# Strassen's seven block products for the first expert product of a fused attention and expert kernel

## The chip, the cores and the metric

One core of one Trainium2 chip runs the whole program in one launch. The metric is the device time of one execution in microseconds (us). Everything is float32; matrix products are exact to about float32 by splitting each operand into a high part (rounded to fp32r, the type that TensorE multiplies) and a low part (the rest), and summing three products: high by low, low by high, high by high.

## The reference

```
x = attention(q, k, v, memory)            # [1152, 512]
h = (x @ w1) * (x @ w2);  x2 = h @ w3 @ w_out   # [1152, 512]
p = probs / probs.sum(-1);  out = 0
for e in range(4):                        # all four experts, every token
    out += p[:, e:e+1] * (relu(x2 @ e_w1[e]) @ e_w2[e])   # 512 -> 1024 -> 512
```

## The kernel before

Tokens are columns: activations are held transposed, features on the 128 partitions, tokens along the free axis, 2 batches of 576 tokens. A first stage (attention, and beside it the product w3 @ w_out) ends in `xT`. `BUnits` (one object per batch) computes (x @ w1) * (x @ w2) in 16 units into `hT`, 8 tiles of 128 features; its matmuls are called `ab` in the trace. `c_unit` multiplies `hT` by the combined weights `Wt` (trace name `c`, 24 matmuls per unit) and evicts: ScalarE copies the high part out of PSUM, VectorE subtracts for the low part (`lo_dve`). Batch 0 goes to `x2a`, batch 1 to `x2b`. The matmuls of batch 1's `ab` and `c` are mixed by the scheduler: a `c` can start on each tile of `hT` that is done.

The expert loop (lines 611 to 660) takes, per expert, three chunks of 512, 384 and 256 tokens (`CHUNKS`). In a chunk the first product (line 622, trace name `d`) makes 8 tiles of 128 hidden features, each from 4 feature blocks by 3 passes (`PASSES`), 12 matmuls; line 628 (ScalarE, relu) and line 629 (VectorE, low part) evict each into `he`. The second product (line 639, trace name `o`) takes 128 tokens at a time as the stationary operand: 8 hidden tiles by 3 passes, 24 matmuls of 512 columns; line 646 or 648 scales by the routing weight and adds to `acc`. Expert weights are loaded once per expert by the DMA queue of SP (line 554), and GpSimd (POOL) makes their high part (`hi_pool`, line 79) and low part (`lo_pool`, line 82). The order on each engine is chosen by the framework's scheduler; each engine then runs its own list in order.

```
for wi, xi in PASSES:
    nc.tensor.matmul(ps, lhsT=ew1[m // 4 * 4 + kk][:, wi, ...], rhs=rhs[:, xi, :], ...)   # L622
nc.scalar.activation(ht[:, 0, :], ps, AF.Relu)                                          # L628
nc.vector.scalar_tensor_tensor(out=ht[:, 1, :], in0=ps, scalar=0.0, in1=r32(ht[:, 0, :]), ...)  # L629
```

Of the kernel before, what the change touches and what calls it, by code (L numbers as in the profile page):

```python
# [33 lines left out]
def kernel(  # L34
# [451 lines left out]
    x2a = [main.tile([P, 2, S], F32R, tag=f"g{d}", name=f"x2a{d}") for d in range(KD)]  # L486
    x2b = []
# [11 lines left out]
    def c_unit(b, d, a, new_ps):  # L499
        st = {}  # L500

        def mm(k0, k1):
            def f():
                if k0 == 0:
                    st["ps"] = new_ps(d, a)
                for kk in range(k0, k1):
                    for x, (wi, xi) in enumerate(PASSES):
                        nc.tensor.matmul(  # L508
                            st["ps"][:, 0:HS], lhsT=Wt[kk][:, wi, d * P : (d + 1) * P],
                            rhs=hT[kk][:, xi, a * HS : (a + 1) * HS],  # L510
                            start=(kk == 0 and x == 0), stop=(kk == KF - 1 and x == 2),
                        )
                if k1 == KF:
                    x2, t0 = (x2b[d], S - CA + a * HS) if b else (x2a[d], a * HS)
                    cut = min(max(C2 - t0, 0), HS) if b else HS
                    for p0, p1, at in ((0, cut, t0), (cut, HS, t0 + cut + SHIFT)):
                        if p0 < p1:
                            ps = st["ps"][:, p0:p1]
                            nc.scalar.copy(x2[:, 0, at : at + p1 - p0], ps)
                            lo_dve(x2[:, 1, at : at + p1 - p0], ps, x2[:, 0, at : at + p1 - p0])  # L520
            return f

        return [mm(k, k + 2) for k in range(0, KF, 2)]

    def ps_main(d, a):
        return psM.tile([P, 512], F32, tag=f"M{a}", name=f"c0_{d}_{a}", bufs=1)
# [16 lines left out]
    fills += spread(C_SLOTS, [c_unit(0, d, a, ps_main) for d in range(KD) for a in range(2)])  # L543
# [8 lines left out]
    def load_tile(pool, rawp, src, tag, nm):  # L552
        r = rawp.tile([P, 512], F32, tag="re", name=f"r{nm}", bufs=3)
        nc.sync.dma_start(out=r, in_=src)
        t = pool.tile([P, 2, 512], F32R, tag=tag, name=nm)
        hi_pool(t[:, 0, :], r)
        lo_pool(t[:, 1, :], r, t[:, 0, :])
        return t

    def load_e1(pool, rawp, e, tag):  # L560

        return [
            load_tile(
                pool, rawp, e_w1[e, k * P : (k + 1) * P, g * 512 : (g + 1) * 512], f"{tag}{4 * g + k}", f"el1{e}_{g}_{k}"
            )
            for g in range(2) for k in range(KD)
        ]
# [26 lines left out]
    pB = p3.enter_context(tc.tile_pool(name="pB", bufs=1, side="left"))  # L594
    ph = p3.enter_context(tc.tile_pool(name="ph", bufs=9, side="left"))
    acc = [main.tile([P, 2, DM], F32, tag=f"g{KD + t}", name=f"acc{t}") for t in range(4)]
    acc.append(pB.tile([P, 1, DM], F32, name="acc4"))
    acc = [acc[t // 2][:, t % 2, :] for t in range(NTT)]
# [8 lines left out]

    groups = [(px, "v"), (main, "u"), (pB, "w")]
    ew2 = load_e2(main, px, 0, "u")
    ng = 2  # L610
    for e in range(E):
        nxt = None
        for c, (c0, cw) in enumerate(CHUNKS):
            hs = []
            x0 = c0 - CA + (SHIFT if c == 2 else 0)
            for m in range(KF):
                ps = ps3.tile([P, 512], F32, tag="P", name=f"d{e}_{c}_{m}")[:, 0:cw]
                n = 0
                for kk in range(KD):
                    rhs = x2a[kk][:, :, c0 : c0 + cw] if c0 < CA else x2b[kk][:, :, x0 : x0 + cw]  # L620
                    for wi, xi in PASSES:
                        nc.tensor.matmul(  # L622
                            ps, lhsT=ew1[m // 4 * 4 + kk][:, wi, m % 4 * P : (m % 4 + 1) * P],
                            rhs=rhs[:, xi, :], start=(n == 0), stop=(n == 3 * KD - 1),
                        )
                        n += 1
                ht = ph.tile([P, 2, 512], F32R, tag="he", name=f"he{e}_{c}_{m}")[:, :, 0:cw]
                nc.scalar.activation(ht[:, 0, :], ps, AF.Relu)  # L628
                nc.vector.scalar_tensor_tensor(  # L629
                    out=ht[:, 1, :], in0=ps, scalar=0.0, in1=r32(ht[:, 0, :]),  # L630
                    op0=ALU.max, op1=ALU.subtract,
                )
                hs.append(ht)
            for tt in range(cw // P):
                po = ps3.tile([P, 512], F32, tag="P", name=f"o{e}_{c}_{tt}")
                n = 0
                for kk in range(KF):
                    for xi, wi in PASSES:
                        nc.tensor.matmul(  # L639
                            po, lhsT=hs[kk][:, xi, tt * P : (tt + 1) * P], rhs=ew2[kk][:, wi, :],  # L640
                            start=(n == 0), stop=(n == 3 * KF - 1),
                        )
                        n += 1
                t = c0 // P + tt
                if e == 0:
                    nc.vector.tensor_scalar_mul(acc[t], po, pr[:, t, e : e + 1])
                else:
                    nc.vector.scalar_tensor_tensor(  # L648
# [47 lines left out]
```

## Time and profile before

| what | us |
|---|---|
| median of 3 runs (lowest to highest) | 757.91 (757.47 to 757.96) |
| the profiled execution's own time | 757.62 |
| its span, first to last instruction | 755.8 |
| TensorE (PE) busy | 737.1, 98% of the span |
| VectorE (DVE), ScalarE (ACT), GpSimd (POOL) busy | 283.9, 235.2, 224.9 |
| expert stage, first `d` matmul to last `o` | 355.87 to 751.69 |

A busy figure is the sum of an engine's instruction times. PE's pipelined matmuls overlap, so its spacing is read from the chain of waits: a stretch of so many matmuls by so many microseconds.

### The profile page before, as it was taken

Reading aid. Unit: us, or ns where it says so; the run is one execution under the profiler, and the core shown is the slowest. Engines: PE = TensorE matmul, PEld = TensorE weight load, DVE = VectorE, ACT = ScalarE, POOL = GpSimd, SP = SyncE. Lnnn points to the kernel's source line nnn. Section 1 sums busy time; section 2 is a strip of 40 time slices with the busy share of each in tenths; the row PEclk is TensorE's granted clock in tenths of the full one; section 3 lists DMA queues with packets and bytes.
Section 4 is the critical chain, followed back from the end, with each engine's and each line's share of the span. In section 5 each row is a group of like instructions: output and inputs, shape, how many; then the busy total and the mean of one; then the engine's idle time right before and its main releaser. Section 6 shows DMA issues by size and latency. Waiting matters only on the chain.

```text
span 755.8 us, 11259 instructions
## 1 busy us (share of the span) xinstructions
PE 737.1 (98%) x4568; PEld 656.1 (87%) x4568; DVE 283.9 (38%) x630; ACT 235.2 (31%) x475; POOL 224.9 (30%) x228
## 2 busy tenths in 40 slices
PE   3899999999999999999999999999999999999997
PEld 2778888899999999999889898898988899888986
DVE  6987557567744125332312122121221212121221
ACT  7976557565734323332201011010111011010110
POOL 2174543544540027003930077000590003400000
PEclk9999999999999999999999999999999999999999
DMA  9873313444511014101420033000131001101010
GB/s 274 277 223 114 105 49 111 146 142 127 180 47 29 2 55 154 56 29 23 138 65 1 1 98 126 0 1 1 57 128 39 1 1 31 39 1 56 0 42 29
DMA packets 48755, 56.69 MB, mean 75 GB/s; under 512 B 15808, under 2 KB 32192, under 8 KB 48704
## 3 DMA queue, kind: packets, MB, share of 16 engines
q1 hardware_dynamic: 48704, 55.97, 24.0%
q8 instruction: 36, 0.59, 0.3%
q14 instruction: 15, 0.12, 0.0%
HBM read 49.41 MB, written 6.55 MB: 74 GB/s over the span
## 4 chain that ended last, share of the span: by engine, by line
PE 92%; ACT 3%; DVE 2%; issue 1%; DMA 0%; POOL 0%; SPq 0%; DVEq 0%; ACTq 0%
PE d L622 26%; PE o L639 26%; PE ab L445 14%; PE c L508 7%; PE a L270 6%; PE wacc L380 5%; PE pt L257 3%; PE sc L217 3%; PE b L294 1%; ACT P L230 1%; PE x L313 1%; DVE tf_l L107 1%; DMA qd<-in_qT_dram 0%; DVE tf_wo L107 0%; ACT tu_l L104 0%
## 5 line engine op out<-in xcount | busy, mean ns | idle before, releaser
L639 PE MATMUL o<-el,he 128*128 128x512 f32 x864 | 198.2, 389 | 0.0
L639 PEld LDWEIGHTS o<-el,he 128*128 128x128 f32 x864 | 161.8, 188 | 33.4
L628 ACT ACTIVATE he<-d 128x512 fp32r<-128x512 f32 (+2 forms) x96 | 47.2, 492 | 337.2 <-PE d L622 337.2
L79 POOL TENSOR_SCALAR el<-rel 128x512 fp32r<-128x512 f32 x64 | 40.3, 636 | 255.5 <-PE d L622 186.3
L622 PE MATMUL d<-x2b,el 128*128 128x384 f32 (+1 forms) x768 | 113.8, 309 | 0.0
L622 PEld LDWEIGHTS d<-x2b,el 128*128 128x128 f32 x768 | 113.2, 188 | 0.6
L445 PE MATMUL ab<-xT,ws 128*128 128x288 f32 x768 | 113.2, 298 | 0.0
L629 DVE SCALAR_TENSOR_TENSOR he<-d,he 128x512 fp32r<-128x512 f32 (+2 forms) x96 | 53.6, 558 | 146.0 <-ACT he L628 146.0
L445 PEld LDWEIGHTS ab<-xT,ws 128*128 128x128 f32 x768 | 104.0, 188 | 1.8 <-ACT P L230 0.2
L622 PE MATMUL d<-x2a,el 128*128 128x512 f32 x384 | 87.7, 389 | 0.0
L622 PEld LDWEIGHTS d<-x2a,el 128*128 128x128 f32 x384 | 72.0, 188 | 14.9
L82 POOL TENSOR_TENSOR el<-rel,el 128x512 fp32r<-128x512 f32 x64 | 83.1, 1314 | 1.8
L648 DVE SCALAR_TENSOR_TENSOR acc<-o,pr,acc 128x512 f32<-128x512 f32 x27 | 20.3, 751 | 123.9 <-PE o L639 123.9
L508 PE MATMUL c<-hT,W 128*128 128x288 f32 x384 | 58.2, 298 | 0.3 <-DVE x2b L85 0.3
L270 PEld LDWEIGHTS a<-v,pT 114*120 114x120 f32 (+1 forms) x480 | 55.1, 193 | 2.6 <-issue 1.5
L270 PE MATMUL a<-v,pT 114*120 114x65 f32 (+1 forms) x480 | 56.2, 276 | 0.0
L508 PEld LDWEIGHTS c<-hT,W 128*128 128x128 f32 x384 | 52.6, 188 | 0.9 <-DVE x2b L85 0.5
L380 PE MATMUL wacc<-wo,w3s 128*128 128x512 f32 x192 | 49.9, 407 | 0.1
L217 PE MATMUL sc<-ks,qs 64*120 64x120 f32 (+5 forms) x288 | 38.1, 377 | 11.9 <-POOL ks L82 9.3
L230 ACT ACTIVATE P<-P,mn 120x120 f32<-120x120 f32 (+3 forms) x80 | 42.5, 580 | 6.1 <-DVE mn L223 5.9
L217 PEld LDWEIGHTS sc<-ks,qs 64*120 64x120 f32 x288 | 25.0, 210 | 20.9 <-POOL ks L82 9.7
L380 PEld LDWEIGHTS wacc<-wo,w3s 128*128 128x128 f32 x192 | 35.9, 193 | 8.1 <-issue 0.9
(76 smaller groups left out, 598.1 us busy)
## 6 DMA issues: line engine op xcount, KB each, us to landing
rel<-in_moe_w_dram SPq DMA_DIRECT2D x64, 256.0 KB, 2.6
wr<-in_moe_w_dram SPq DMA_DIRECT2D x16, 512.0 KB, 3.8
w3r<-in_moe_w3T_dram SPq DMA_DIRECT2D x16, 512.0 KB, 4.2
wor<-in_moe_w_out_dram SPq DMA_DIRECT2D x8, 512.0 KB, 6.4
wf<-tf SPq DMA_DIRECT2D x16, 256.0 KB, 2.2
wr<-wf SPq DMA_DIRECT2D x16, 256.0 KB, 3.1
v<-in_v_dram SPq DMA_DIRECT2D x16, 150.0 KB, 3.9
qd<-in_qT_dram SPq DMA_DIRECT2D x8, 288.0 KB, 3.5
```

The lines of the kernel that those rows point to most:

```text
L79: nc.gpsimd.tensor_scalar(out=dst, in0=src, scalar1=1.0, scalar2=1.0, op0=ALU.mult, op1=ALU.mult)
L82: nc.gpsimd.tensor_sub(dst, src, r32(hi))
L217: nc.tensor.matmul(ps[x][:, c : c + k1 - k0], lhsT=qs[o, a, q0[i] : q0[i] + RP], rhs=ks[o, b, k0:k1], start=(m == 0), stop=(m == 2),)
L230: nc.scalar.activation(Pt[i], Pt[i], AF.Exp, bias=mn[:, i : i + 1], scale=-1.0)
L270: nc.tensor.matmul(st["a"][:, x, i, :], lhsT=pt[x, i, j][0 : rows[j]], rhs=vn[0 : rows[j], j, :], start=(j == 0), stop=(j == i),)
L380: nc.tensor.matmul(wacc[t], lhsT=w3s[u][:, a, c, :], rhs=wo[4 * g + c][:, bb, :], start=(g == 0 and c == 0 and x == 0), stop=(g == 1 and c ...
L445: nc.tensor.matmul(ps[:, 0:HS], lhsT=self.ws[u][:, wi, kk, :], rhs=xT[b, kk][:, xi, a * HS : (a + 1) * HS], start=(n == 0), stop=(n == 3 * ...
L508: nc.tensor.matmul(st["ps"][:, 0:HS], lhsT=Wt[kk][:, wi, d * P : (d + 1) * P], rhs=hT[kk][:, xi, a * HS : (a + 1) * HS], start=(kk == 0 an ...
L622: nc.tensor.matmul(ps, lhsT=ew1[m // 4 * 4 + kk][:, wi, m % 4 * P : (m % 4 + 1) * P], rhs=rhs[:, xi, :], start=(n == 0), stop=(n == 3 * KD ...
L628: nc.scalar.activation(ht[:, 0, :], ps, AF.Relu)
L629: nc.vector.scalar_tensor_tensor(out=ht[:, 1, :], in0=ps, scalar=0.0, in1=r32(ht[:, 0, :]), op0=ALU.max, op1=ALU.subtract,)
L639: nc.tensor.matmul(po, lhsT=hs[kk][:, xi, tt * P : (tt + 1) * P], rhs=ew2[kk][:, wi, :], start=(n == 0), stop=(n == 3 * KF - 1),)
```

## The change

The first product of an expert is done as Strassen's block scheme (the form with seven products that share sums). The 512 input features are two halves, the 1024 hidden features two halves, and the tokens two halves, the two batches; a "step" makes one pair of hidden tiles (features f and f + 512) for both batches. Tokens are cut into column pieces of 320 and 256 per batch (`COLS`). There are 4 experts by 2 pieces by 4 pairs = 32 steps. A step has seven products of 2 feature blocks by 3 passes, 6 matmuls each, 42 in all of 320 or 256 columns, into three PSUM banks Z, Q and R; four of the products accumulate on Z one after the other, and ScalarE copies Z out (`s1`, `u2`, `u3`) between them. The copies are added by VectorE to R or Q (`t11`, `t22`, `t12`) before relu and split.

The activations' sums T1 to T4 are made once per piece by VectorE (`combine_x`), each then split into high and low. The weights' sums S1 to S4 are made for each step by POOL from freshly loaded weights (`prep_1`), so weights are loaded for each piece, twice as often; ScalarE now makes the high parts of all expert weights and VectorE the low part of the second product's (`prep_2`). PE's order is written by hand from here on: a step's seven products with the second product of the preceding step cut into five pieces between them. The first step has the remaining `c` matmuls of batch 1 (the 256-column piece) there instead. `lo_dve`, `lo_pool` and `PASSES` are as before.

```diff
-    CHUNKS = ((0, 512), (512, 384), (896, 256))
+    COLS = ((0, 320), (320, 256))
...
                 if k1 == KF:
-                            nc.scalar.copy(x2[:, 0, at : at + p1 - p0], ps)
-                            lo_dve(x2[:, 1, at : at + p1 - p0], ps, x2[:, 0, at : at + p1 - p0])
+                    nc.scalar.copy(x2[b][d // 2][:, d % 2, t0 : t0 + tw], st["ps"])
...
+    def combine_x(c):
+        b11, b21, b12, b22 = (block(n, c) for n in ("B11", "T4", "T1", "B22"))
+        return [
+            *split_x("B22", c),
+            lambda: sub(t, b22, b12), lambda: sub(b12, b12, b11), lambda: sub(b22, b22, b12), lambda: sub(b21, b21, b22),
+            *split_x("T2", c), *split_x("T1", c), *split_x("T3", c), *split_x("T4", c),
+        ]
...
+        return [begin, hi(0), lo(0), s31, hi(2), s24, hi(3), hi(1), lo(2), lo(1), lo(3)]
...
+    early = [f for n in ("B11", "B21") for c in range(2) for f in split_x(n, c)]
+    early += prep_1(0)
...
+    for d in range(KD):
+        for f in c1(d, 0, d):
+            f()
+    c1_rest = [f for d in range(KD) for f in c1(d, 1, (KD + d) % 5)]
...
+        prod(Z, "A11", "B11", True)
+        nc.scalar.copy(s1, Z)
+        prod(R, "A12", "B21", True)
+        nc.vector.tensor_add(t11, s1, R)
+        relu_split(h0[:, :, 0:w], t11)
+        seg()
+        prod(Z, "S2", "T2", False)
+        nc.scalar.copy(u2, Z)
+        prod(Q, "S1", "T1", True, 0, 1)
+        seg()
+        prod(Z, "S3", "T3", False)
+        nc.scalar.copy(u3, Z)
+        prod(Q, "S1", "T1", True, 1, 2)
+        nc.vector.tensor_add(t22, u3, Q)
+        relu_split(h1[:, :, w : 2 * w], t22)
+        seg()
+        prod(Z, "A22", "T4", False)
+        relu_split(h1[:, :, 0:w], Z)
+        seg()
+        prod(Q, "S4", "B22", False)
+        nc.vector.tensor_add(t12, u2, Q)
+        relu_split(h0[:, :, w : 2 * w], t12)
+        seg()
...
+    with tc.manual_schedule(engines={mybir.EngineType.PE}):
+        segs = cut(c1_rest, 4) + [[]]
+        for s in range(len(steps)):
+            load_1(s + 2)
+            if s == 0:
+                step(s, segs)
+                queue += [(0, f) for f in (*prep_2(0), *prep_2(1), *combine_x(1))]
+                pop(0, 5)
+            else:
+                load_2(s + 1)
+                step(s, cut(layer2(s - 1), 5))
+                queue += [(s + 1, f) for f in prep_2(s + 1)]
+            queue += [(s + 2, f) for f in prep_1(s + 2)]
+        for f in layer2(len(steps) - 1):
+            f()
```

`seg()` emits the next piece of the second product and up to six of the queued preparations; `relu_split` is a relu on ScalarE and the low part on VectorE, as lines 628 and 629.

PE before, at the end of batch 1's `c` and the start of the experts (`x2a` holds batch 0, `el1` the weights):

```order
L508 MATMUL c1_3_1_4032<-hT1_5_3241,W5_65 128x288 x3
L508 MATMUL c1_3_1_4032<-hT1_6_3242,W6_66 128x288 x3
L508 MATMUL c1_3_1_4032<-hT1_7_3243,W7_67 128x288 x3
L622 MATMUL d0_0_0_4122<-x2a0_146,el10_0_0_3798 128x512 x3
L622 MATMUL d0_0_0_4122<-x2a1_147,el10_0_1_3803 128x512 x3
```

The first chunk's tokens are all of batch 0, done long before. PE now, at the same place, in the first step (Z0 and Q0 are its banks, X0T2 and X0T1 the split sums T2 and T1 of the 320-column piece, w11 and w12 the weights' sums):

```order
L506 MATMUL c1_1_0_3853<-hT1_7_3247,W7_67 128x320 x3
L506 MATMUL c1_2_0_3879<-hT1_7_3247,W7_67 128x320 x3
L506 MATMUL c1_3_0_3905<-hT1_7_3247,W7_67 128x320 x3
L506 MATMUL c1_0_1_4032<-hT1_6_3246,W6_66 128x256 x2
L506 MATMUL c1_0_1_4032<-hT1_7_3247,W7_67 128x256 x3
L793 MATMUL Z0_4005<-X0T2_3227,w11_0_3508 128x320 x6
L793 MATMUL Q0_4006<-X0T1_3226,w12_0_3509 128x320 x3
L506 MATMUL c1_1_1_4068<-hT1_0_3240,W0_60 128x256 x3
```

Five `c` matmuls stand between the last 320-column result of batch 1 (`c1_3_0`) and the first matmul that reads T2. VectorE now, at the same place (L575 are the sums, L82 the low parts of a split; x2_11 and x2_10 are batch 1's halves):

```order
L575 TENSOR_TENSOR t3_3238<-x2_11_149,x2_10_148 128x640
L82 TENSOR_TENSOR X0B22_3230<-x2_11_149,X0B22_3230 128x640
L575 TENSOR_TENSOR x2_10_148<-x2_10_148,x2_00_146 128x2x320
L82 TENSOR_TENSOR X0T3_3228<-t3_3238,X0T3_3228 128x640
L575 TENSOR_TENSOR x2_11_149<-x2_11_149,x2_10_148 128x2x320
L82 TENSOR_TENSOR X0T1_3226<-x2_10_148,X0T1_3226 128x640
L575 TENSOR_TENSOR x2_01_147<-x2_01_147,x2_11_149 128x2x320
L82 TENSOR_TENSOR X0T2_3227<-x2_11_149,X0T2_3227 128x640
L82 TENSOR_TENSOR X0T4_3229<-x2_01_147,X0T4_3229 128x640
L816 TENSOR_TENSOR t22_0_4014<-u3_0_4012,Q0_4006 128x320
```

All of it is new, and T2's low part is the eighth. VectorE at the end of the first step (he0 is its output, in the parts t11, t22, Z and t12; L725 the low part after relu; X1... the 256-column piece):

```order
L575 TENSOR_TENSOR t3_3238<-x2_11_149,x2_10_148 128x2x256
L823 TENSOR_TENSOR t12_0_4015<-u2_0_4011,Q0_4006 128x320
L82 TENSOR_TENSOR X1B22_3237<-x2_11_149,X1B22_3237 128x512
L725 SCALAR_TENSOR_TENSOR he0_0_4008<-t11_0_4013,he0_0_4008 128x320
L575 TENSOR_TENSOR x2_10_148<-x2_10_148,x2_00_146 128x2x256
L725 SCALAR_TENSOR_TENSOR he0_1_4009<-t22_0_4014,he0_1_4009 128x320
L725 SCALAR_TENSOR_TENSOR he0_1_4009<-Z0_4005,he0_1_4009 128x320
```

The read of bank Z, which the next step's first product overwrites, stands last of these seven, behind the sums of the second piece. After it come six more such 512-wide operations, three small ones on the routing weights and one relu low part, and then the second step's `t11`.

## Rows read from the trace of the kernel before

**Rows 1.** Page, parts 1 and 4: engines; the chain's shares by line.
```profile
PE 737.1 (98%) x4568; PEld 656.1 (87%) x4568; DVE 283.9 (38%) x630; ACT 235.2 (31%) x475; POOL 224.9 (30%) x228
PE d L622 26%; PE o L639 26%; PE ab L445 14%; PE c L508 7%; PE a L270 6%; PE wacc L380 5%; PE pt L257 3%; PE sc L217 3%; PE b L294 1%; ACT P L230 1%; PE x L313 1%; DVE tf_l L107 1%; DMA qd<-in_qT_dram 0%; DVE tf_wo L107 0%; ACT tu_l L104 0%
```
**Rows 2.** Chain that ended last: start us, us, engine, name, line, count.
```profile
301.28 3.18 PE ab L445 x24
...
348.03 7.83 PE c L508 x57
355.87 21.78 PE d L622 x96
377.65 21.76 PE o L639 x96
399.41 16.75 PE d L622 x96
...
432.53 11.37 PE d L622 x96
...
740.72 10.94 PE o L639 x48
751.69 0.75 DVE acc L648
```
**Rows 3.** Groups by shape: busy us, mean ns, idle before. DVE, ACT, POOL.
```profile
L629 DVE SCALAR_TENSOR_TENSOR he<-d,he 128x384 fp32r<-128x384 f32 x32 | 17.9, 558 | 50.5 <-ACT he L628 50.5
L629 DVE SCALAR_TENSOR_TENSOR he<-d,he 128x256 fp32r<-128x256 f32 x32 | 13.6, 425 | 32.3 <-ACT he L628 32.3
...
L628 ACT ACTIVATE he<-d 128x384 fp32r<-128x384 f32 x32 | 15.8, 492 | 137.9 <-PE d L622 137.9
L628 ACT ACTIVATE he<-d 128x256 fp32r<-128x256 f32 x32 | 12.3, 384 | 98.2 <-PE d L622 98.2
L435 ACT CAST ws<-wr 128x512 fp32r<-128x512 f32 x16 | 10.0, 623 | 7.8 <-PE ab L445 7.1 <-issue 0.7
...
L82 POOL TENSOR_TENSOR el<-rel,el 128x512 fp32r<-128x512 f32 x64 | 83.1, 1314 | 1.8
```
**Rows 4.** Timeline, 282 to 302 us: start, us, engine, line, operation.
```profile
282.79 2.99 POOL L82 TENSOR_TENSOR el<-rel,el 128x512 fp32r<-128x512 f32 x2
283.07 1.56 DVE L85 TENSOR_TENSOR ws<-wr,ws 128x512 fp32r<-128x512 f32 x1 [3.24 <-ACT ws L435]
...
299.36 0.69 DVE L85 TENSOR_TENSOR ws<-wr,ws 128x512 fp32r<-128x512 f32 x1 [3.37 <-ACT ws L435]
...
301.35 0.46 DVE L85 TENSOR_TENSOR hT<-asb,hT 128x288 fp32r<-128x288 f32 x1 [0.50 <-ACT hT L496]
```
**Rows 5.** Timeline, hand-overs from PE to ACT and from ACT to DVE.
```profile
355.70 6.53 PE L622 MATMUL d<-x2a,el 128*128 128x512 f32 x28
358.71 0.60 ACT L628 ACTIVATE he<-d 128x512 fp32r<-128x512 f32 x1 [1.99 <-PE d L622]
...
561.97 0.60 ACT L628 ACTIVATE he<-d 128x512 fp32r<-128x512 f32 x1 [2.12 <-PE d L622]
562.60 0.69 DVE L629 SCALAR_TENSOR_TENSOR he<-d,he 128x512 fp32r<-128x512 f32 x1 [2.03 <-ACT he L628]
```
**Rows 6.** Timeline of PE before 60 us; a window at the end (third-last column: PEclk).
```profile
42.25 4.04 PE L380 MATMUL wacc<-wo,w3s 128*128 128x512 f32 x12
...
54.88 5.50 PE L380 MATMUL wacc<-wo,w3s 128*128 128x512 f32 x23
754.50:755.80 1.30, 0.00 (x0) 0.00 (x0) 0.00 (x0) 0.00 (x0) 0.00 (x0) 0.50 0.00 0
```
**Rows 7.** Timeline at the start of batch 1's `ab`; DMA issues, us to landing.
```profile
276.27 0.64 ACT L316 CAST xT<-x 128x576 fp32r<-128x576 f32 x1 [0.63 <-PE x L313]
278.74 8.23 PE L445 MATMUL ab<-xT,ws 128*128 128x288 f32 x60
...
wr<-wf SPq DMA_DIRECT2D x16, 256.0 KB, 3.1
```

More of the change, by code (lines that the diff above doesn't have):

```diff
@@ L483 @@
         f()
-    x2a = [main.tile([P, 2, S], F32R, tag=f"g{d}", name=f"x2a{d}") for d in range(KD)]
-    x2b = []
+    x2 = [
+        [main.tile([P, 2, S], F32, tag=f"g{2 * b + k}", name=f"x2_{b}{k}") for k in range(2)] for b in range(B)
+    ]
     def new_h(b):
@@ L550 @@
     attn.close()
[L552 to L567, printed above, removed]
@@ new lines, in prep_2, with begin @@
+    def prep_2(s):
+        if s >= len(steps):
+            return []
+        st = {}
+        def begin():
+            st["r"] = raw2.pop(s)
+            w2s[s] = [
+                main.tile([P, 2, DM], F32R, tag=f"u{(2 * s + x) % KF}", name=f"w2_{s}_{x}") for x in range(2)
+            ]
+        return [
+            begin,
+            *(lambda x=x: nc.scalar.copy(w2s[s][x][:, 0], st["r"][:, x]) for x in range(2)),
+            *(lambda x=x: lo_dve(w2s[s][x][:, 1], st["r"][:, x], w2s[s][x][:, 0]) for x in range(2)),
+        ]
@@ L591 @@
     p2.close()
[L594 to L598, printed above, removed]
+    pB = p3.enter_context(tc.tile_pool(name="pB", bufs=1, side="left", reuse_waits="tile"))
+    WM = COLS[0][1]
+    TILES = 5
     pr = pB.tile([P, NTT, E], F32, name="pr")
@@ new lines, in temp, with rows_of @@
+    def temp(nm, s, w):
+        pool = pB if nm in ("t11", "t12") else pC
+        return pool.tile([P, WM], F32, tag=nm, name=f"{nm}_{s}", bufs=2)[:, 0:w]
+    acc = [main.tile([P, 2, DM], F32, tag=f"g{KD + t}", name=f"acc{t}") for t in range(4)]
+    acc.append(acc4)
+    acc = [acc[t // 2][:, t % 2, :] for t in range(NTT)]
+    def rows_of(t):
+        c, i = divmod(t, TILES)
+        t0, w = COLS[c]
+        spans = []
+        for b in range(B):
+            lo, hi = max(i * P, b * w), min((i + 1) * P, (b + 1) * w)
+            if lo < hi:
+                spans.append((lo - i * P, hi - i * P, b * S + t0 + lo - b * w))
+        return spans
@@ new lines, in cut, with pop, step, prod @@
+    def cut(fs, n):
+        k = [len(fs) * i // n for i in range(n + 1)]
+        return [fs[k[i] : k[i + 1]] for i in range(n)]
+    queue = []
+    def pop(s, n):
+        while n and queue and queue[0][0] <= s + 2:
+            queue.pop(0)[1]()
+            n -= 1
+    def step(s, segs):
+        e, c, j = steps[s]
+        w = COLS[c][1]
+        Z = psM.tile([P, 512], F32, tag="M0", name=f"Z{s}", bufs=1)[:, 0:w]
+        Q = psM.tile([P, 512], F32, tag="M1", name=f"Q{s}", bufs=1)[:, 0:w]
+        R = ps3.tile([P, 512], F32, tag="R", name=f"R{s}")[:, 0:w]
+        h0, h1 = h_of[s] = [new_he(s, x, w) for x in range(2)]
+        s1, u2, u3 = (temp(n, s, w) for n in ("s1", "u2", "u3"))
+        t11, t22, t12 = (temp(n, s, w) for n in ("t11", "t22", "t12"))
+        def prod(ps, a, b, first, k0=0, k1=2):
+            for kk in range(k0, k1):
+                for x, (wi, xi) in enumerate(PASSES):
+                    nc.tensor.matmul(
+                        ps, lhsT=w1s[s][a][:, wi, kk, :], rhs=X[c, b][:, xi, kk, :],
+                        start=first and kk == 0 and x == 0, stop=(kk == 1 and x == 2), skip_group_check=True,
+                    )
+        def seg():
+            for f in segs.pop(0):
+                f()
+            pop(s, 6)
+        prod(Z, "A11", "B11", True)
[21 more added lines that the diff above has]
+        seg()
@@ L606 @@
     nc.vector.tensor_mul(pr, pr, prs.unsqueeze(2).to_broadcast([P, NTT, E]))
[L608 to L648, printed above, removed]
-                        out=acc[t], in0=po, scalar=pr[:, t, e : e + 1], in1=acc[t], op0=ALU.mult, op1=ALU.add
-                    )
-                if e == E - 1:
-                    nc.sync.dma_start(out=out[t * P : (t + 1) * P, :], in_=acc[t])
-            if c == 0 and e + 1 < E:
-                pool, tag = groups[ng % 3]
-                ng += 1
-                nxt = load_e1(pool, px, e + 1, tag)
-        if e + 1 < E:
-            pool, tag = groups[ng % 3]
-            ng += 1
-            ew1, ew2 = nxt, load_e2(pool, px, e + 1, tag)
```

172 lines of the change are left out of this document (142 added, 30 removed).

## The prediction

> **What bounds the kernel now.** I read the page's engine shares first: PE is busy for 98% of the span, and 52% of the chain that ended last is the two expert products, `d` and `o` [rows 1]. Then the chain in order of time [rows 2]: from 355.87 us to 751.69 it is nothing but stretches of `d` and `o`, one starting where the last ends. So the expert stage is a dense stream of matmuls, and only fewer columns, or a new gap, can move it. The chain also gives the spacing of a matmul by its width: 512 columns 21.76 / 96 = 0.2267 us, 384 columns 16.75 / 96 = 0.1745, 288 columns 3.18 / 24 = 0.1325, 256 columns 11.37 / 96 = 0.1184 [rows 2]. Last I read the other engines by shape, since the change gives them new work in front of PE's [rows 3 to 5].
>
> A change of under 0.2% (1.5 us) cannot be told from none here. The sum is made against the profiled execution's own 757.62 us, 0.3 below the median.
>
> **What the stream gains.** Before, `d` is 1152 matmuls, per expert 21.76 + 16.75 + 11.37 = 49.88 us, 199.5 in all [rows 2]. After, it is 16 steps of 42 matmuls of 320 columns and 16 of 42 of 256: 1344 narrower ones. 320 columns lie between 288 and 384, a third of the way: 0.1465 us (bounds 0.1325 and 0.1745). 672 x 0.1465 + 672 x 0.1184 = 178.0. **Gain 21.5 us**. The second product keeps its 864 matmuls of 512 columns. Batch 1's `c` goes from 192 of 288 columns (25.4 us) to 96 of 320 and 96 of 256 (25.4): nothing.
>
> **The steady step, costed at nothing.** A 320 step takes PE 42 x 0.1465 + 30 x 0.2267 = 12.96 us, a 256 step 42 x 0.1184 + 24 x 0.2267 = 10.4. Beside it stand: POOL, 3 subtractions of 512 at 1.31 [rows 3] and 5 of 256, which by width are about half of that, 7.2 us; ACT, three copies and four relus at 0.38 to 0.44, five casts of 512 at 0.62 and one of 256, 6.6; DVE, 3 sums, 4 low parts of relu at 0.43 to 0.49 and 2 low parts of 512 at 0.69 [rows 3, 4], 4.8, with five additions to `acc` of 0.75 [rows 2] in every fourth step. None fills the step. What could be late is a copy of bank Z, because the next product on Z waits for it. ACT takes up a result some 0.25 us after PE (0.29 in [rows 5]: twelve matmuls from 355.70 end at 358.42, the relu starts at 358.71), DVE 0.03 after ACT [rows 5]. In a 256 step the tightest chain runs: two weight casts and a relu left from the step before, `s1`, their low parts on DVE, `t11`, its relu, `u2`; added up it ends 4.0 us into the step, and PE wants Z at 4.5. So PE is covered, by 0.5 us; in a 320 step by 1.1. DMA carries twice the weights, by their shapes 33.6 MB in some 390 us or 86 GB/s, two steps ahead: hidden.
>
> **What the switchover costs.** Four places, in PE's order. A two-input operation on DVE goes 0.46 us at 288 columns and 0.69 at 512 [rows 4], so 0.82 at 640.
>
> *A, start of batch 1's `ab`.* ACT now makes four casts of the B blocks (0.7 and 0.6 each) and a weight cast before it empties the first `ab` bank, and that cast waits for a load that can start only with the cast of `xT`, at 276.3 [rows 7]. Before, the cast of `xT` ends at 276.91, and PE wants the bank at 278.74 + 24 x 0.1325 = 281.9 [rows 7]. Casts and a copy take 3.7 us, and some 1.2 more if the load needs the 3.1 us of its nearest kind [rows 7], to 279.4: bank free between 281 and 282.3. Then low parts and POOL's eight first operations meet on DVE (below), and `c` can no longer step in until `hT`'s first tile is whole. From 0 to 2.5 us; I take 1.5, nearer the upper, since POOL runs without pause there.
>
> *B, the first T2.* PE reaches it 5 x 0.118 = 0.6 us after the last 320-column `c`. T2's low part, which the first pass reads, is DVE's eighth operation there: 0.25 + 0.43 (copy) + 8 x 0.82 = 7.3 us. PE waits 6.7. If one or two POOL operations (1.3 each) get in between, 8.0 or 9.3. I take 7.4: one of them is ready in mid chain, at even odds.
>
> *C, bank Z for the second step.* The last `c` ends 0.88 us (6 x 0.1465) before PE wants Z again. DVE first does the six operations listed ahead of the read of Z, from 0.7 us on: 0.69 + 0.47 + 0.69 + 0.49 + 0.69 + 0.49 + 0.49 = 4.0, so 4.7 - 0.9 = 3.8. With one POOL subtraction in it 5.1. I take 4.4.
>
> *D, `u2` of the second step.* Behind that read stand 6 x 0.69 + 0.49 + 0.66 on DVE, then `t11` (0.49); then ACT's relu, two casts and the copy, 2.1: 7.9 us, and PE wants it after 6 + 6 + 6 + 3 narrow and 12 wide matmuls, 5.8. Wait 2.1. POOL has three or four operations to do in that stretch (2.6 to 3.9): up to 6.0. I take 3.4, since some fit beside single-input operations.
>
> Before, nothing like B to D exists: the first chunk reads only batch 0, and `c` runs into `d` without a gap [rows 2].
>
> *The lock.* Where POOL subtracts and DVE has a two-input operation, both stretch: DVE took 1.56 us for what takes 0.69 alone, POOL 2.99 for two of 1.31 [rows 4]. That is one waiting for the other, and the contended ends above use it. The Trainium skill (SBUF — State Buffer, Who interferes with whom) has this as an exclusive lock, held for a whole instruction, and only for a DVE instruction whose inputs are both in SBUF. By that page the three sums with a PSUM input stay free and three of the relu low parts, which now read SBUF, do not; by the row alone one could not say.
>
> *F, the clock.* The granted clock is 0.50 (1.2 GHz) in the last 1.3 us, after the last matmul ended at about 751.7 [rows 6]. So a gap of 2.8 us was enough for a fall, and B is longer. For the price I have 12 matmuls of 512 in 4.04 us early on against 23 in 5.50 [rows 6]: 1.2 us lost on regaining speed. One fall surely, a second at even odds: 1.8 (0 to 3.6). The Trainium skill (TensorE: Matmul & The Clock Gate, Why this matters for your kernels) says that PE must not stand idle for long or it drops to half rate; by it C and D may fall too, 3.6 instead of 1.8, and the time 756.4.
>
> **Sum.** 757.62 - 21.5 + 1.5 + 7.4 + 4.4 + 3.4 + 1.8 = **754.6 us**. With all lower ends (0, 6.7, 3.8, 2.1, 0) 748.7; with all upper ones (2.5, 9.3, 5.1, 6.0, 3.6) 762.6. I expect most of Strassen's gain to be paid back at the switchover.
>
> **Rivals.** *Hidden after all:* the waits B to D stay under 9 us, because DVE's operations are shorter than their widths say. For it: the steady stream. Against: eight operations in a row cannot be overlapped with each other. 757.6 - 21.5 + 10 = 746, at the extreme 738.
>
> *All ends contended:* POOL gets in everywhere and the clock falls three times: 757 to 762.6. For it: POOL's queue is never empty there. No change, or a little slower.
>
> *Slower, by the lock in every step:* the place is `u2` in the 256 steps, with 0.5 us to spare. If one POOL subtraction of 1.31 gets in front of the two low parts that `t11` stands behind, PE waits 0.8 us in each of 16 steps, 13 in all: 767. From 0.2 us per 256 step on, the forecast's 3 us are gone. For it: DVE's two-input work and POOL's add up to 9.8 of 10.4 us in such a step. Against: POOL has to wait for the next weight cast just then. It is the place where the skill's rule of the lock bites, by 13 us.
>
> *Narrower matmuls save no time:* with bank and weights changing more often a matmul could cost more than its width. Against: 256 columns ran at 0.1184 in groups of 12 [rows 2]. 1 us per 60 matmuls would make it 757 or worse.
>
> **How the numbers follow.** Forecast, 748.7 to 756.1: 0.45. Hidden: 0.10. All contended: 0.20, of which 0.16 lie within 1.5 us of no change. Lock in every step: 0.20, of which 0.02 within. Narrow matmuls: 0.05, slower. Faster by over 0.2%: 0.55; within: 0.18; slower: 0.27. The range takes in half of the hidden case and the nearer part of the slower ones: 745 to 764.
>
> **What would show it.** `d`'s line replaced by 1344 matmuls at 0.1465 and 0.1184 spacing; PE gaps of 6.7 us or more with DVE's X0T2 as releaser, of about 4 with DVE's read of Z0, of 2 to 6 with ACT's `u2`; granted clock 0.50 for some us behind the first; 12.96 and 10.4 us per step afterwards. Steps longer than that, with PE waiting for ACT's `u2` copy, would make the forecast wrong upward; no gap at X0T2, wrong downward.

## The result, and the profile after

The changed kernel takes **761.85 us** (median of 4 runs, 761.53 to 763.31) against 757.93 (757.47 to 757.97) before, a ratio of 1.0057 with a 95% interval of 1.0039 to 1.0074: slower by some 0.6%. The forecast was 754.6 with a range of 745 to 764, and faster as the likeliest sign. The profiled execution took 761.87 us, 7.3 over the forecast.

The page after, parts 1, 2 and 4 (engines; TensorE's granted clock in 40 slices; the chain's shares by engine and by line), which answers to [rows 1]:

```profile
PE 722.8 (95%) x4760; PEld 651.2 (86%) x4760; DVE 414.0 (54%) x824; ACT 383.4 (50%) x801; POOL 354.4 (47%) x356
...
PEclk9999999999999999998889999999999999999999
...
PE 87%; DVE 5%; ACT 4%; DMA 1%; issue 1%; SPq 1%; POOL 0%; DVEq 0%; ACTq 0%; POOLq 0%
PE o L739 26%; PE Z L793 13%; PE ab L442 13%; PE Q L793 7%; PE c L506 6%; PE a L267 6%; PE wacc L377 5%; PE R L793 3%; PE sc L214 3%; PE pt L254 3%; PE b L291 1%; DVE tf_l L104 1%; ACT P L227 1%; DMA r<-in_moe_w_dram 1%; DVE x L575 1%
```

PE has 14 us less work and the span is 4.3 us longer. DVE and ACT are now on the chain, and the clock is down at one place, slices 19 to 21. There lie PE's three long waits. Timeline of PE after (start us, us, what, and in brackets the idle time before it):

```profile
357.66 1.97 PE L793 MATMUL Z<-X0T,w 128*128 128x320 f32 x6 [7.02 <-ACT X0T L563]
...
378.03 1.97 PE L793 MATMUL Z<-X0B,w 128*128 128x320 f32 x6 [5.61 <-DVE he L725]
...
387.74 1.54 PE L793 MATMUL Z<-X0T,w 128*128 128x320 f32 x6 [2.04 <-ACT u L810]
```

These are the forecast's B (named after ACT's high part, but DVE's low part of the same tile ends last), C and D, at the places named. Six such matmuls take 1.04 us in a steady step (below), and up to 1.97 here. Windows after (busy us per engine; the third-last column is the granted clock):

```profile
354.20:360.90 6.70, 3.24 (x13) 3.24 (x14) 4.23 (x5) 2.50 (x4) 2.86 (x4) 0.50 0.28 81
374.70:381.40 6.70, 3.37 (x13) 3.37 (x13) 6.70 (x11) 2.72 (x6) 2.82 (x3) 0.50 0.75 235
388.30:391.60 3.30, 3.30 (x13) 2.91 (x12) 3.30 (x4) 1.35 (x3) 3.30 (x4) 0.50 0.38 132
345.00:400.00 55.00, 40.33 (x237) 37.72 (x237) 35.59 (x49) 30.01 (x62) 31.96 (x29) 0.84 0.28 84
```

At half rate PE was busy 3.24 + 3.37 + 3.30 = 9.9 us, so it did work of 5.0 us in twice the time. Behind 400 us it never waits, and yet eight steps (one expert) take 94.7 us where the forecast has 4 x 12.96 + 4 x 10.4 = 93.4. Timeline of PE after, in a 320 step:

```profile
506.23 1.56 PE L739 MATMUL o<-w,he 128*128 128x512 f32 x6
507.63 1.04 PE L793 MATMUL Z<-X0T,w 128*128 128x320 f32 x6
508.50 0.61 PE L793 MATMUL Q<-X0T,w 128*128 128x320 f32 x3
508.94 1.54 PE L739 MATMUL o<-w,he 128*128 128x512 f32 x6
510.32 1.05 PE L793 MATMUL Z<-X0T,w 128*128 128x320 f32 x6
```

From start to start: nine narrow ones (320 columns; 512 are called wide) take 508.94 - 507.63 = 1.31, 0.1456 each, as forecast; six of `o` 1.40 and 1.38, 0.232 each, where 512 columns took 0.2267 before [rows 2]. Over all starts between 400 and 735 us the mean distance is 0.2323 for `o` after, 0.2271 before; 0.1467 for 320 columns and 0.1184 for 256. So two things were to be explained: the long `o`, and the switchover.

### The profile page after: what moved, and what is told of

Same layout as the page of the kernel before. It is cut to its first block, busy times and chain, and to the rows that moved or that the text cites. A ratio compares the mean times of both kernels' runs of the same rounds, so it can differ in the third digit from the quotient of the medians.

```text
span 760.1 us, 12572 instructions
## 1 busy us (share of the span) xinstructions
PE 722.8 (95%) x4760; PEld 651.2 (86%) x4760; DVE 414.0 (54%) x824; ACT 383.4 (50%) x801; POOL 354.4 (47%) x356
## 4 chain that ended last, share of the span: by engine, by line
PE 87%; DVE 5%; ACT 4%; DMA 1%; issue 1%; SPq 1%; POOL 0%; DVEq 0%; ACTq 0%; POOLq 0%
PE o L739 26%; PE Z L793 13%; PE ab L442 13%; PE Q L793 7%; PE c L506 6%; PE a L267 6%; PE wacc L377 5%; PE R L793 3%; PE sc L214 3%; PE pt L254 3%; PE b L291 1%; DVE tf_l L104 1%; ACT P L227 1%; DMA r<-in_moe_w_dram 1%; DVE x L575 1%
## 5 line engine op out<-in xcount | busy, mean ns | idle before, releaser
L739 PE MATMUL o<-w,he 128*128 128x512 f32 x864 | 226.7, 395 | 0.0
L79 POOL TENSOR_TENSOR w<-r,w 128x512 fp32r<-128x512 f32 x96 | 129.4, 1349 | 152.7 <-ACT w L628 152.7
L739 PEld LDWEIGHTS o<-w,he 128*128 128x128 f32 x864 | 154.7, 189 | 24.8
L725 DVE SCALAR_TENSOR_TENSOR he<-t,he 128x320 fp32r<-128x320 f32 (+1 forms) x96 | 71.3, 742 | 40.5 <-ACT he L724 40.5
L628 ACT CAST w<-r 128x512 fp32r<-128x512 f32 x96 | 59.3, 619 | 49.4 <-PE Q L793 20.6
L724 ACT ACTIVATE he<-t 128x320 fp32r<-128x320 f32 (+1 forms) x96 | 42.4, 443 | 35.8 <-DVE t L806 19.0
L793 PE MATMUL Z<-X0T,w 128*128 128x320 f32 x288 | 51.4, 315 | 9.1 <-ACT X0T L563 7.0
L793 PEld LDWEIGHTS Z<-X0T,w 128*128 128x128 f32 x288 | 46.8, 192 | 13.6 <-DVE X0T L82 7.2
L82 DVE TENSOR_TENSOR w<-r,w 128x512 fp32r<-128x512 f32 x64 | 51.9, 834 | 11.7 <-ACT w L658 11.7
L506 PE MATMUL c<-hT,W 128*128 128x288 f32 (+2 forms) x384 | 56.2, 299 | 0.4 <-DVE hT L82 0.4
```

What stands on the lines that cost most here:

```text
L79: nc.gpsimd.tensor_sub(dst, src, r32(hi))
L82: nc.vector.tensor_sub(dst, src, r32(hi))
L506: nc.tensor.matmul(st["ps"], lhsT=Wt[kk][:, wi, d * P : (d + 1) * P], rhs=hT[kk][:, xi, t0 : t0 + tw], start=(kk == 0 and x == 0), stop=(k ...
L628: return lambda: nc.scalar.copy(st["w"][i][:, 0], src(i))
L725: nc.vector.scalar_tensor_tensor(out=h[:, 1], in0=src, scalar=0.0, in1=r32(h[:, 0]), op0=ALU.max, op1=ALU.subtract)
L739: nc.tensor.matmul(o_ps[i], lhsT=h_of[s][x][:, a, i * P : (i + 1) * P], rhs=w2s[s][x][:, b, :], start=first, stop=last,)
```

## The experiments

The first four take the readings that lay nearest: that a change from narrow to wide costs something per piece of `o`, and that each wait costs a fall of the clock on top.

**1. All of `c`'s rest first.**

```diff
-        segs = cut(c1_rest, 4) + [[]]
+        segs = [c1_rest, [], [], [], []]
```

> Edit: all sixteen pieces of the last four c1 products (11.4 us of TensorE at full rate) run in the first place of step 0, ahead of S2*T2, and none in the later places. The same work in another order. Theory (the first wait of 7.0 us stands there only because 2.9 us of ready work covered DVE's chain of eight operations, and a fall of the clock of 1.7 us comes with it): the wait for X0T2 goes, and with it its fall; small waits of a few tenths appear behind it, where u2 and u3 have no cover left; w2's and combine_x(1)'s operations start earlier. 752.5 to 755, that is 7 to 9 us under the changed kernel's 761.9. Rival (the wait only moves: to T3's operand, to the copies u2 and u3, or to the second step's Z, where DVE is as full as before): 758.5 to 762.

Measured: 752.03 (751.61 to 753.79), ratio to before 0.9929 (0.9917 to 0.9941): 9.8 us under the changed kernel, and faster than before. PE's waits in it (us in total, times, longest):

```profile
PE Q L793 <- DVE t L816: 3.1, 1, 3.1
...
PE Z L793 <- DVE he L725: 1.4, 1, 1.4
...
PE Z L793 <- ACT u L814: 0.9, 2, 0.7
PE Z L793 <- ACT u L810: 0.6, 1, 0.6
```

The 7.0 is gone, the 5.6 has shrunk to 1.4, and a new wait of 3.1 for `t` has come. The 5.6 shrinks because of what DVE does next. Its first low part of `w2` (timelines, the first row of the changed kernel, the second of this one):

```profile
369.93 2.57 DVE L82 TENSOR_TENSOR w<-r,w 128x512 fp32r<-128x512 f32 x3 [4.42 <-ACT w L658]
```
```profile
358.42 2.72 DVE L82 TENSOR_TENSOR w<-r,w 128x512 fp32r<-128x512 f32 x2 [0.53 <-ACT w L658]
```

`w2` goes into the buffers of `W`, the weights of `c`, and the second column piece's sums need `c`'s results: both can start only when `c` is through or nearly so. With `c` ahead of the wait the first starts 11.5 us earlier, and the second piece's first sum 10.1 (at 363.34 us, not 373.42).

**2 and 3. Fewer and more pieces of `o`.** Two (with the halves of S1 x T1 together), then ten (products split between them; `more()` emits a piece).

```diff
...
-                step(s, cut(layer2(s - 1), 5))
+                m = cut(layer2(s - 1), 2)
+                step(s, [[], [], m[0], [], m[1]])
```
```diff
-                step(s, cut(layer2(s - 1), 5))
+                step(s, cut(layer2(s - 1), 10))
...
+        more()
```

> Edit: from the second step on, o's matmuls stand in two pieces per step, not five, and the two halves of S1*T1 together. The same work. Theory (each piece of wide matmuls between narrow ones costs TensorE 0.03 to 0.05 us, which no wait shows): 3 pieces fewer in 31 steps, 93 times 0.03 to 0.05 = 2.8 to 4.7 us, so 757.2 to 759.1. Rival (the 1.2 us by which eight steps were longer than the sum of their matmuls come from something else, such as single matmuls that start late because weights or operands are late): 761.5 to 762.5, or above, where a copy u2 that has only 0.9 us of cover is now waited for.

> Edit: from the second step on, o's matmuls stand in ten pieces per step, not five; the order of the products is unchanged. Theory (0.03 to 0.05 us for each piece of wide matmuls between narrow ones): 5 pieces more in 31 steps, 155 times 0.03 to 0.05 = 4.7 to 7.8 us more than 761.9, so 766.6 to 769.7, spread evenly over the steps, with no wait in the list of TensorE's waits. Rival (the excess does not go with the number of pieces): 761.4 to 762.4.

Measured: two pieces 768.34 (765.73 to 770.0), slower; ten 764.59 (763.3 to 765.38), 2.7 over the changed kernel and short of 4.7. The theory falls. Timeline with two pieces, then with ten:

```profile
502.77 3.66 PE L739 MATMUL o<-w,he 128*128 128x512 f32 x15
506.26 1.04 PE L793 MATMUL Z<-X0B,w 128*128 128x320 f32 x6
...
519.41 0.87 PE L793 MATMUL Z<-X1B,w 128*128 128x256 f32 x6
...
523.09 3.66 PE L739 MATMUL o<-w,he 128*128 128x512 f32 x15
```
```profile
507.59 0.86 PE L739 MATMUL o<-w,he 128*128 128x512 f32 x3
508.29 1.04 PE L793 MATMUL R<-X0B,w 128*128 128x320 f32 x6
```

Fifteen in a row take (506.26 - 502.77) / 15 = 0.2327 each, three 0.70 / 3 = 0.233. It is a price per wide matmul, not per piece. With ten pieces the steady steps last as long as with five (13.11 us from the start of one step's product into bank R to the next step's); its 2.7 us lie in the first two steps (37.3 and 18.5 us against 34.8 and 17.7). With two, thirty 256-column matmuls in a row took 523.09 - 519.41 = 3.68, 0.1227 each and not 0.1184. That is not a price of long rows: [rows 2] has 96 in a row at 0.1184. The excess stands at two places of the thirty: from the 13th start to the next pass 0.194 us and from the 25th 0.188, on the mean of the steps between 400 and 735 us, elsewhere 0.117 to 0.121. The 13th and the 25th are each the first of a further product into bank Z. Timeline with two pieces (PEld loads the weights):

```profile
520.37 0.37 ACT L804 COPY s<-Z 128x256 f32<-128x256 f32 x1
520.80 0.77 PEld L793 LDWEIGHTS Z<-X1T,w 128*128 128x128 f32 x6
...
521.87 0.36 ACT L810 COPY u<-Z 128x256 f32<-128x256 f32 x1
522.28 0.76 PEld L793 LDWEIGHTS Z<-X1T,w 128*128 128x128 f32 x6
```

The load comes 0.05 to 0.06 us after ACT's copy of Z ends: with no piece of `o` ahead of it, PE waits there for the copy, some 0.07 us each time, which the list of waits does not show. The prediction named the copies of Z as what could be late in a 256 step. They make 0.15 us in each of 16 steps; with 1.7 us in the first two steps that makes up the profiled execution, the fastest of its runs; the rest up to its median no row shows.

**4. The waits filled with idle work** (`fill`: matmuls into a free bank; 43 before S2 x T2, 34 before the second step, 12 before its S3 x T3).

```diff
+        def fill(ps, lhsT, rhs, n):
+            for i in range(n):
+                nc.tensor.matmul(ps, lhsT=lhsT, rhs=rhs, start=i == 0, stop=i == n - 1)
```

> Edit: TensorE gets idle work in the three places in which it waited: 43 matmuls of 320 columns (6.3 us) before S2*T2 of step 0, 34 (5.0 us) before the first product of step 1, 12 (1.8 us) before S3*T3 of step 1, each into a bank that is free there. They leave the result as it is and save nothing; they end before what was waited for comes. Theory (each wait brought a fall of the clock that cost 1.7 us on top of it): with the clock kept up 1.7 us come back per wait that is filled, 5 in all if the second and third waits don't grow by what is won ahead of them, so 756.5 to 760, and the granted clock stays at 1.0 from 345 to 400 us. Rival (the half rate cost nothing of itself, because DVE was the later one there anyway): 761.4 to 763, with the waits longer by what TensorE won.

Measured: 761.88 (761.73 to 764.98), clock 0.998 over the span, nothing gained. The first step is 3.1 us shorter (31.7 from R to R, not 34.8), the next two 1.5 and 1.3 longer: PE comes earlier and waits for `u` (2.5 us) and `s` (0.6). That is the rival's case, but the third fill stood in the way itself; run 14 repeats it without.

**5 and 6. The order on DVE, and on ACT, as the program names it** (on top of run 1).

```diff
-    with tc.manual_schedule(engines={mybir.EngineType.PE}):
+    with tc.manual_schedule(engines={mybir.EngineType.PE, mybir.EngineType.DVE}):
```

> Edit: the order of the first experiment (all c1 pieces ahead of S2*T2), and DVE keeps the order in which the program names its work, as TensorE does, so that t22, t12 and the low parts of he come ahead of the second column block's combinations. Theory (what is left of the switchover, 3.1 us for t22 and 1.4 us for he, is DVE's order, not its load): both waits go, 745.5 to 748. Rival (DVE, ACT and POOL are all full there, and the wait comes back as one for a weight, or for u behind a cast on ACT): 750.5 to 753.

> Edit: as the run before, and ACT keeps the program's order too, so that the copies u2 and u3 stand ahead of casts of weights that wait for POOL. Theory (the waits for u are such casts, as the fourth experiment's trace shows for 2.5 us): the waits for u shrink to under 0.3 each, 0.5 to 1.5 us under the run before. Rival (casts that come later make POOL's low parts later, and the steps' weights are late): the same time as the run before, or above it by 1 us or more with waits of Z or R for w in many steps.

Measured: 755.64 (754.14 to 757.73) and 777.92 (775.63 to 781.92). Both miss. With DVE's order the first step is 6.6 us shorter than in run 1 (21.4), the second and third 5.5 and 2.5 longer, with 3.6 us for `he` again and 1.5 for `w`: the wait moves. With ACT's order too, PE waits for `he` 18 times, 24.2 us in all, nearly all of it in the steady steps. The scheduler's order, with casts where there is room, was the better one.

**7. The wide matmul by itself**: fifteen series behind the last product.

```diff
+        series("A", 30, *own, banks=5)
+        series("B", 30, *own)
+        series("C", 30, hcol(0), wcol(0))
...
+        series("E", 30, hcol(32), wcol(0))
...
+        series("H", 30, hcol(0), wcol(32))
...
+        series("O", 60, *own)
```

> Edit: the changed kernel with fifteen series of wide matmuls behind its last product, each into a bank that is free, so that nothing of the result changes; twelve narrow ones stand ahead of each but one. A: o's own operands, a new bank every six. B: the same in one bank. C to G: one weight tile, shifted by 0, 8, 32, 64, 96 columns. H, I: the moving tile shifted by 32 and 128. J, K: weights from the first product's tiles. L: a moving tile X. M: nothing narrow ahead. N: narrow ones of 384 columns. O: sixty in a row. It is about 480 wide and 170 narrow ones, 130 us more, so 885 to 900 us; what counts is the distance of starts in each series. Theory 1 (where operands lie decides): some of C to L have 0.2267 and others 0.232, and B, M and O are as A. Theory 2 (the narrow ones ahead leave TensorE in a state that wide ones keep): M, which follows wide ones, and the end of O have 0.2267, the beginnings of the others 0.232. Theory 3 (the bank change every six): A alone 0.232, B 0.2267. Theory 4 (the work of the other engines beside it): all 0.2267, since nothing else runs there.

Measured (a single execution, 891.52 us): timeline of PE in it.

```profile
757.82 7.13 PE L871 MATMUL serA<-w,he 128*128 128x512 f32 x30
764.78 1.59 PE L862 MATMUL narrow<-X1B,w 128*128 128x256 f32 x12
...
791.44 6.98 PE L871 MATMUL serE<-w,he 128*128 128x512 f32 x30
798.26 1.60 PE L862 MATMUL narrow<-X1B,w 128*128 128x256 f32 x12
...
808.11 7.01 PE L871 MATMUL serG<-w,he 128*128 128x512 f32 x30
814.96 1.60 PE L862 MATMUL narrow<-X1B,w 128*128 128x256 f32 x12
...
816.40 6.97 PE L871 MATMUL serH<-w,he 128*128 128x512 f32 x30
823.21 1.60 PE L862 MATMUL narrow<-X1B,w 128*128 128x256 f32 x12
...
874.74 14.11 PE L871 MATMUL serO<-w,he 128*128 128x512 f32 x60
```

A takes 6.96 / 30 = 0.232, E and H 6.82 and 6.81, 0.227, G 6.85. Single starts show that E has the long distance three times, G nine times, H once, and then 0.2267 to the end. All others have 0.232 to 0.234 throughout: B in one bank, D (shifted by 32 bytes), F (256 bytes), I (512 bytes), M with nothing narrow ahead, and O to its sixtieth. Nothing else runs there, so theories 2 to 4 fall. What E, G and H share is the place: by the program's allocation `he` lies 64 bytes above a multiple of 256 there and `w2` 192 above (in short, at 64 and 192 modulo 256). E and G move the weights by 128 and 384 bytes, H what moves by 128; in these three alone both lie alike modulo 256. J and K have their weights at 64 and `w2` at 192, L has `he` at 64 and a moving tile at 160: apart, and long. In the kernel before both are 192 above.

**8, 9 and 10. The place alone.** An unused tile ahead of `he` made 128 bytes smaller or larger in the changed kernel, larger in the one before.

```diff
-    pB.tile([P, 224], F32, name="pad")
+    pB.tile([P, 192], F32, name="pad")
```
```diff
-    pB.tile([P, 224], F32, name="pad")
+    pB.tile([P, 256], F32, name="pad")
```
```diff
-    pB.tile([P, SHIFT], F32, name="gapB")
+    pB.tile([P, SHIFT + 32], F32, name="gapB")
```

> Edit: the unused tile pad ahead of he is 32 floats smaller, so that he (the weights of o) lies 128 bytes lower and w2 (what moves) stays: both then at 192 modulo 256, where they were at 64 and 192. Not one instruction changes. Theory (the 864 wide matmuls of o cost 0.2323 us, not 0.2267, because of how he and w2 lie to each other): 864 times 0.0056 = 4.8 us less than 761.9, so 757 to 758.5 if a new stretch has the short distance at once; 759.5 to 761.5 if the first three to ten matmuls of a stretch keep the long one, as series E and G of the seventh experiment did, since a piece has only four to six. Rival (the long distance comes from alternating with narrow matmuls): 761.4 to 762.4.

> Edit: the same unused tile 32 floats larger, he 128 bytes higher: he at 448 and w2 at 192 modulo 512, so equal modulo 256 as in the run before, and apart modulo 512, as in series E of the seventh experiment (three long distances, then short ones) and in the kernel before. Theory: 757 to 760.5, and whichever of this and the run before has the shorter start of a piece is the faster. Rival: 761.4 to 762.4.

> Edit: the kernel before, with 32 floats more in the unused tile ahead of he: he and the third group of weight tiles lie 128 bytes higher, so that for the experts 0, 1 and 3 the weights of o are at 64 and what moves is at 192 modulo 256, as in the changed kernel. No instruction changes. Theory (where they lie sets the distance): 648 matmuls of o at 0.2323 in place of 0.2271 and the 96 wide first products of expert 1 too: 3.4 to 4.2 us over 757.7, so 761 to 762. Rival (only alternating with narrow matmuls does it): 757.4 to 758.1.

Measured: 759.96 (758.4 to 761.65) and 760.11 (758.68 to 760.75), 1.9 and 1.7 us less than the changed kernel; the kernel before 762.35 (761.85 to 763.33), ratio 1.0064 (1.0051 to 1.0078), 4.5 us more. No instruction differs. (The pad also moves the first product's weights of every third step; their narrow matmuls change by about 0.001 us or less.) Timeline of run 9, then the chain of run 10 in order of time:

```profile
504.46 1.52 PE L739 MATMUL o<-w,he 128*128 128x512 f32 x6
505.83 1.05 PE L793 MATMUL Z<-X0T,w 128*128 128x320 f32 x6
```
```profile
378.23 22.32 PE o L639 x96
...
456.56 22.30 PE d L622 x96
478.86 22.32 PE o L639 x96
...
579.02 21.77 PE o L639 x96
```

In run 10 the experts whose `he` and weights now lie apart take 22.32 / 96 = 0.2325 (0.2267 in [rows 2]), as does expert 1's wide first product; expert 2, whose weights moved along, stays at 21.77. In run 9 six of `o` take 1.37, not 1.40: the first two of a piece keep 0.231, the rest have 0.2288 to 0.2274, 0.2294 on the mean. So a piece of four to six is too short: 864 x (0.2323 - 0.2294) = 2.5 us come back, and some 0.6 of them are lost again, because the first narrow matmul behind a piece takes 0.1505 (320 columns) or 0.1215 (256) in place of 0.1472 and 0.1172, 155 times.

**11 and 12. Together** (runs 1 and 9), and then three pieces of `o`.

```diff
+                m = cut(layer2(s - 1), 3)
+                step(s, [[], m[0], m[1], [], m[2]])
```

> Edit: the two that helped, together: all c1 pieces ahead of S2*T2, and he 128 bytes higher. Theory (one acts in the switchover, the other in the steady steps, so they add): 752.0 less 1.8 = 750.2, between 749.5 and 751. Rival (he's place costs as much elsewhere, since pools above it move too): 751.5 to 752.5.

> Edit: as the run before, and from the second step on o's matmuls in three pieces (ten or eight each), not five, the products in the same order. Theory (with he higher only the first two of a piece take 0.231 and the rest 0.2273 to 0.2288, so a piece more costs some 0.013 us): two pieces fewer in 31 steps, 0.8 us less, 749 to 750. Rivals (as with two pieces, narrow matmuls in a longer row get slower; or the copies and t have too little cover): 0 to 3 us more than the run before.

Measured: **749.47** (748.96 to 750.28), ratio to before 0.9892 (0.9877 to 0.9908), 12.4 us under the changed kernel: they add (9.8 and 1.7 would be 11.5), and this version beats both. Three pieces: 752.8 (751.09 to 753.03), 3.3 over run 11 and not 0.8 under it; in rows of twenty-one 256-column matmuls the 13th waits for the copy of Z as in run 2, and `t` is waited for 5.9 us at the switchover, not 3.1.

**13 and 14. The clock once more**: idle work in two waits of run 11 (19 and 8 matmuls), and in the first two waits of the changed kernel (43 and 26).

```diff
+        if s == 1:
+            fill("C", 8)
...
+        if s == 0:
+            fill("Q", 19)
```
```diff
+        if s == 1:
+            fill("C", 26)
...
+        if s == 0:
+            fill("B", 43)
```

> Edit: the eleventh experiment's kernel with idle matmuls where it still waits longest: 19 of 320 columns (2.8 us) before S4*B22 of step 0, where 3.1 us stood, and 8 (1.2 us) before the first product of step 1, where 1.4 us stood. They save nothing of themselves. In that kernel TensorE then ran 10.2 us at half rate. Theory (the half rate makes TensorE the late one there): with the clock kept up the time falls by 2 to 4.5 us, to 745 to 747.5. Rival (DVE, ACT and POOL set the end of the switchover, and what TensorE wins it waits for u, s or t a little later): 748.7 to 750.3.

> Edit: the changed kernel with idle matmuls in the first two waits alone, 43 (6.3 us) and 26 (3.8 us of 5.6), and none at the third, so that no idle work can be in the way. Theory: the two falls of 1.7 us go and are won, 758 to 759.5, with the wait for u no longer than 2.0 us. Rival: the waits for u and s grow by what was won, 761 to 762.5, as with all three filled.

Measured: 754.03 (753.95 to 755.42), 4.6 us above run 11, and 761.18 (760.72 to 761.32), 0.7 under the changed kernel. In run 14 the first step is 3.3 us shorter (31.55), the second and third 0.4 and 1.6 longer: of the 3.3 us that the two falls seemed to cost, 1.2 are won. Its waits, and what ACT does ahead of the longest:

```profile
PE Z L801 <- ACT u L824: 2.8, 1, 2.8
...
PE Z L801 <- ACT s L812: 1.2, 1, 1.2
```
```profile
386.59 0.62 ACT L628 CAST w<-r 128x512 fp32r<-128x512 f32 x1 [1.98 <-POOL r L641]
387.11 0.42 ACT L824 COPY u<-Z 128x320 f32<-128x320 f32 x1
```

This `u` (L824) is `u3`; it stands on ACT behind a cast that waits for POOL. The framework's scheduler sets ACT's order, and with the idle work in the program it set another one: in the changed kernel PE waits for `u2`, behind casts without such a wait, and `u3` is there in time. So the runs show that keeping the clock up does not bring the 5 us back here; what a fall costs by itself they do not.

## Why the prediction was wrong

Right: the stream's gain (0.1467 and 0.1184 against 0.1465 and 0.1184), the three waits with their places and causes, and that most of the gain would be paid back at the switchover. By term, in us:

| term | forecast | measured |
|---|---|---|
| A, `ab` and `c` waiting (0.2 and 0.4 in the list of waits; before, 0.3) | 1.5 | 0.6 |
| B, T2 | 7.4 | 7.0 |
| C, bank Z | 4.4 | 5.6 |
| D, `u2` | 3.4 | 2.0 |
| F, half rate | 1.8 | 5.0 |
| steady steps, `o` | 0 | 864 x (0.2323 - 0.2271) = 4.5 |
| ahead of `ab` (279.75 us, 278.74 in [rows 7]) | 0 | 1.0 |

The differences add up to -0.9 - 0.4 + 1.2 - 1.4 + 3.2 + 4.5 + 1.0 = 7.2 of the 7.3 us. Each is good to a few tenths only: A takes nothing off for the 0.3 before, and from start to start B, C and D are up to 0.2 longer than the idle times listed.

**The step that failed is "The steady step, costed at nothing"**, in the sentence before it: "The second product keeps its 864 matmuls of 512 columns." It keeps them, but not their distance. `he` and `w2` came to lie at different offsets modulo 256 bytes, and each wide matmul takes 2.3% longer. Runs 7 and 10 show that, and runs 8 and 9 give part of it back: 2.5 of the 4.5 us go with the place, and 2.0 stay (0.2294 against 0.2271), because cutting `o` into short pieces makes the start of a stretch come again and again. Without the 4.5 us the profiled execution would have been at 757.4, level with the 757.62 before, so this step alone does not bring the forecast's gain back. The rival "narrower matmuls save no time" was near in that it doubted the price of a matmul, but it looked at the narrow ones and at changes of bank and weights, which cost nothing here (0.1467 and 0.1184). Its price was wrong as well: 1 us per 60 of 1344 matmuls is 22 us, and 757 needs only 1 us in some 560.

**The second is F, mis-sized**: one sure fall and one at even odds, 1.2 us each, against three of 1.7. The Trainium skill (TensorE: Matmul & The Clock Gate, Why this matters for your kernels), by which C and D fall too, had the count right, though the third fall stands behind a wait of 2.0 us, shorter than the gaps that the section warns of. Runs 4, 13 and 14 change what F means: PE's lost time was largely cover for the other engines, and sums of waits and falls as separate costs overstate what removing one of them brings. Which engine of the three sets the length of the switchover is not settled; orders on DVE and ACT only moved the wait.

That the time lies within 745 to 764, and within the 757 to 762.6 of "all ends contended", is luck: B, C and D add up to 14.7 us, less than the 15.2 forecast and far from that rival's 20.4, and only its three falls came true. The rest came from F and from `o`, for which the sum had no term.

What I did not see at all is that `c` heads the chain. B was priced as a wait of PE. Run 1 shows that it held up the rest of `c`, and so everything that needs `c`'s end; moving work that had been there anyway won 9.8 us.

The 1.0 us ahead of `ab` belongs mostly to this execution: no run on the changed kernel alters anything ahead of it, and in the others `ab` starts at 278.92 to 279.44 us (278.97 in run 1). What made it late no row shows.

The lock did stretch DVE at the switchover, but in the 256 steps PE waits for nothing, so that rival (767) failed (in run 2, with less cover, PE does wait for the copies there, 0.07 us at a time). Timelines of POOL and DVE in run 4:

```profile
387.11 3.06 POOL L79 TENSOR_TENSOR w<-r,w 128x512 fp32r<-128x512 f32 x2
...
388.16 0.49 DVE L830 TENSOR_TENSOR t<-u,Q 128x320 f32<-128x320 f32 x1 [0.36 <-ACT u L828]
389.18 1.34 DVE L725 SCALAR_TENSOR_TENSOR he<-t,he 128x320 fp32r<-128x320 f32 x1 [0.54 <-ACT he L724]
```

Beside two POOL operations the sum with an input in PSUM takes its usual 0.49, the relu low part with both inputs in SBUF 1.34. That is the rule of the Trainium skill that the forecast weighed (SBUF — State Buffer, Who interferes with whom), and the trace agrees.

## What to carry to other kernels

Read the spacing of matmuls that a change does not touch: where tiles come to lie is part of a change, and here a pad of 128 bytes was worth 1.9 us in one kernel and 4.5 in the other. When an engine waits at a change of stages, look for work that it has anyway and that other engines' next work depends on, and put that in the gap; idle work that keeps the clock up won 0.7 us in one place and lost 4.6 in another. Waits and half rate in one stretch overlap with the same work of the other engines: price the chain that ends the stretch, not each gap.

## What was not expected of the hardware

A matmul of 512 columns starts 0.2267 us after the one ahead when its weights and its moving tile begin at the same offset modulo 256 bytes, and 0.232 to 0.234 when not (pairs 64 and 192, 96 and 192, 64 and 160; other distances were not tried). The offsets are those of the program's allocation; that a shift of one operand by 128 or 384 bytes brings the short distance, and one of 32, 256 or 512 does not, run 7 shows by itself. Coming from narrower matmuls, the short distance sets in only after one, three or nine matmuls (series H, E, G), in the kernel before after ten. The Trainium skill (SBUF — State Buffer, Who interferes with whom) gives TensorE two read ports, one for what moves and one for weights, and calls them independent; by that the place would not matter. Here it does, by 2.3%, and the measurement decides. What inside makes the difference no run shows. Whether the narrow products would gain from another place of X (160 modulo 256, its weights at 192 or 64) was not tried.
